# Moving the table load, the ranking and the weight conversions in a fused attention, expert and gated-product kernel

## The chip, the core and the metric

The kernel runs on one core of a Trainium2 chip. The metric is the device time of one execution in microseconds (us). Three executions of the kernel before took 904.47, 911.55 and 910.23 us; the median is 910.23 us.

## What is computed

Three layers follow each other. The first is a gated linear attention with 4 batches, 8 heads, 768 steps and head width 48. The second sends each of the 3072 tokens to one of 8 experts (two matrices 384x1024 and 1024x384). The third is a gated product with 1536 hidden columns.

```python
f = 1 / (1 + exp(-f_logit))
for t in range(S):                                   # attention
    state = f[:, :, t, :, None] * state + einsum('bhd,bhe->bhde', k[:, :, t], v[:, :, t])
    y[:, :, t] = einsum('bhd,bhde->bhe', q[:, :, t], state)
logits = xn @ en.T / tau                             # routing, x and expert rows normalised
expert_idx = argmax(logits); gate_w = softmax(logits)[expert_idx]
for e in range(E):
    out[mask] = gate_w[mask] * (relu(x[mask] @ w1[e]) @ w2[e])
return ((x @ w_a) * (x @ w_b)) @ w_out               # gated product
```

## The kernel before

The order of the instructions on each engine is the order in which the program writes them; every engine works through its own list in order. DMAs are issued from SP's and ACT's lists, the scatters from POOL's.

**Attention.** The time axis is cut into 24 blocks g (6 chunks of 128 steps times 4 batches). `load_a(g)` fetches q, k and f of a block in two halves, one issued by SP and one by ACT; `load_b(g)` fetches two forms of v on SP. `prep_f(g)` makes the forget gates on ACT (a Tanh and a Copy), `prep_s(g)` runs two scans and five other operations on DVE, which make `kt` and `qc`. `pe(g)` is the block's PE work: the products `pp` of block g+2, the part of `y(g)` that comes from the state (`inter`), the part from within the block (`intra`), the products `kv` of block g+1 and the state's update `u_ps`. `evac(g)` copies y out of PSUM and squares it for the norm. In the loop, block g sees `prep_f(g+4)`, `prep_s(g+3)` and `pe(g)`. Ahead of the loop stand the constants, `warm_up` matmuls on a zero tile, `prep_f(0..3)`, `prep_s(0..2)` and two `pe` calls.

**Routing.** After the blocks 3, 7, 11, 15, 19, 21 and 23, `route` ranks the tokens of the round. It is a generator: `tick` writes its next piece between the pieces of `prep_s` and `pe`. `until(k)` holds it back until the loop counter `it` has reached the round's block plus k; `it` is raised by one for each block, and by a half in the middle of `pe`. Its matmuls `rk` give the positions, `pz`, `pos` and further small DVE operations follow, then the gate; `scale_row` and `scatter_row` write the rows to DRAM by expert.

**Experts.** 64 steps (8 experts, 8 slices of hidden columns): `h_part`, `h_split`, `y_part`. Products are made in three passes from a high and a low part of each operand, so the weights are converted: ACT makes the high part, POOL or DVE subtracts it to get the low part.

**Gated product.** 72 steps (6 tiles of 512 tokens, 12 slices of hidden columns). `ab_part(s)` makes two products `pa`, multiplies them on DVE (`rows`, L913) and splits the result into `gh` (ACT) and `gl` (DVE); `q_part(s-1)` is the second product, whose passes take `gh` and `gl` of the step before. The gated weights come as 64-bit numbers; `job_run` converts one half piece in three stages, each advanced by `w_next`: an Abs on ACT and three DVE operations, two DVE operations, then the high part on ACT and the low part (`lo`, L691) on POOL. Nine of the eighteen half pieces are converted in the first gated steps.

Of the kernel before, what the change touches and what calls it, by code (L numbers as in the profile page):

```python
# [6 lines left out]
F32 = mybir.dt.float32  # L7
F32R = mybir.dt.float32r
BF16 = mybir.dt.bfloat16
I32 = mybir.dt.int32  # L10
ACTF = mybir.ActivationFunctionType
# [38 lines left out]
def build(tc, I, out, dbg=None):  # L50
# [12 lines left out]
    ident = const.tile([128, 128], F32, name="ident")  # L63
    off_i = const.tile([1, NE], I32, name="off_i")
    ones = const.tile([128, 128], BF16, name="ones")
    warm = const.tile([128, 512], BF16, name="warm")
    flag_i = const.tile([1, 1], I32, name="flag_i")
    flag_b = const.tile([1, 1], BF16, name="flag_b")
    fl_sb = const.tile([128, 1], F32, name="fl_sb")
# [49 lines left out]
    with tc.manual_schedule():  # L119
# [178 lines left out]
        def warm_up(n):  # L298
            wp = ps_kv.tile([128, 512], F32, tag="kv", name="wp")
            for i in range(n):  # L300
                T.matmul(out=wp, lhsT=ones, rhs=warm, start=(i == 0), stop=(i == n - 1))

        def pe(g):
            n = g + 2
# [26 lines left out]

        def evac(g, y, rd):
            i = len(rd["x"])
            yx = x_p.tile([128, H, VW], F32, tag="yx", name="yx", bufs=7)
            A.activation(out=yx, in_=y, func=ACTF.Copy)
            junk = x_p.tile([128, H, D], BF16, tag="junk", name="junk", bufs=1)
            A.activation(out=junk, in_=yx[:, :, 0:D], func=ACTF.Square, accum_out=rd["ssq"][:, i:i + 1])
            late.append(lambda: V.tensor_reduce(out=rd["lg"][:, i], in_=yx[:, :, D:VW].rearrange("p h e -> p e h"),
                                                axis=AX.X, op=ALU.add))
            rd["x"].append((g, yx))  # L340
# [5 lines left out]
        def route(rd, i0):  # L346
            nb = len(rd["x"])
            lg, ssq = rd["lg"][:, 0:nb], rd["ssq"][:, 0:nb]
            rt = lambda nm, w=NE, dt=F32: r_p.tile([128, B, w], dt, tag=nm, name=nm)[:, 0:nb]
            bc = lambda t: t.to_broadcast([128, nb, NE])  # L350
            prio_b = prio.unsqueeze(1).to_broadcast([128, nb, NE])

            def until(k):
                while it[0] < i0 + k:
                    yield

            yield from until(1)
            nrm = rt("nrm", 1)
            G.tensor_tensor(out=nrm[:, :, 0], in0=ssq, in1=half[:, 0:nb], op=ALU.pow)
            mx = rt("mx", 1)  # L360
            V.tensor_reduce(out=mx, in_=lg, axis=AX.X, op=ALU.max)
            yield
            eq = rt("eq")
            V.tensor_tensor(out=eq, in0=lg, in1=bc(mx), op=ALU.is_ge)
            z = rt("z")
            V.tensor_tensor(out=z, in0=lg, in1=bc(mx), op=ALU.subtract)
            yield
            V.tensor_tensor(out=eq, in0=eq, in1=prio_b, op=ALU.mult)
            yield
            m2 = rt("m2", 1)  # L370
            V.tensor_reduce(out=m2, in_=eq, axis=AX.X, op=ALU.max)
            yield
            oh = rt("oh", NE, BF16)
            V.tensor_tensor(out=oh, in0=eq, in1=bc(m2), op=ALU.is_equal)
            yield from until(2)
            ps = ps_r.tile([128, B, NE], F32, tag="r", name="rk")[:, 0:nb]
            T.matmul(out=ps, lhsT=tri, rhs=oh, start=True, stop=False, skip_group_check=True)
            T.matmul(out=ps, lhsT=ones[0:1], rhs=base[:, 0:nb], start=False, stop=False, skip_group_check=True)
            T.matmul(out=ps, lhsT=ones, rhs=run.unsqueeze(1).to_broadcast([128, nb, NE]),
                     start=False, stop=(nb == 1), skip_group_check=True)  # L380
            for i in range(nb - 1):
                T.matmul(out=ps[:, i + 1:nb], lhsT=ones,
                         rhs=oh[:, i:i + 1].to_broadcast([128, nb - 1 - i, NE]),
                         start=False, stop=(i == nb - 2), skip_group_check=True)
            V.tensor_scalar(out=nrm, in0=nrm, scalar1=1e-6, scalar2=None, op0=ALU.add)
            yield
            V.reciprocal(out=nrm, in_=nrm)
            yield
            V.tensor_tensor(out=z, in0=z, in1=bc(nrm), op=ALU.mult)
            yield from until(2.5)  # L390
            A.activation(out=z, in_=z, func=ACTF.Tanh, scale=0.5)
            yield
            pz = rt("pz")
            V.tensor_tensor(out=pz, in0=ps, in1=oh, op=ALU.mult)
            yield
            pos = rt("pos", 1)
            V.tensor_reduce(out=pos, in_=pz, axis=AX.X, op=ALU.add)
            yield
            seen = r_p.tile([128, NE], F32, tag="seen", name="seen")
            V.tensor_reduce(out=seen, in_=oh.rearrange("p i e -> p e i"), axis=AX.X, op=ALU.add)  # L400
            yield
            V.tensor_tensor(out=run, in0=run, in1=seen, op=ALU.add)
            yield
            posi = r_p.tile([128, B, 1], I32, tag="posi", name="posi", bufs=4)[:, 0:nb]
            V.tensor_copy(posi, pos)
            yield from until(3)
            den = rt("den")
            V.tensor_scalar(out=den, in0=z, scalar1=-1.0, scalar2=1.0, op0=ALU.mult, op1=ALU.add)
            yield
            V.reciprocal(out=den, in_=den)  # L410
            yield
            V.scalar_tensor_tensor(out=den, in0=z, scalar=1.0, in1=den, op0=ALU.add, op1=ALU.mult)
            yield
            gate = rt("gate", 1)
            V.tensor_reduce(out=gate, in_=den, axis=AX.X, op=ALU.add)
            yield
            V.tensor_scalar(out=gate, in0=gate, scalar1=1e-9, scalar2=None, op0=ALU.add)
            yield
            V.reciprocal(out=gate, in_=gate)
            for i, (g, yx) in enumerate(rd["x"]):  # L420
                scq.append((g, yx, gate[:, i], posi[:, i]))
# [56 lines left out]
        SP.dma_start(out=en_bd, in_=I["embbd"])  # L478
        tau = ob_p.tile([128, 1], F32, name="tau")
        V.memset(half, 0.5)  # L480
        V.memset(ones, 1.0)
        V.memset(warm, 0.0)
        V.memset(qkf_t[1], 0.0)
# [4 lines left out]
        SP.dma_start(out=tau, in_=I["tau"].to_broadcast([128, 1]))  # L488
        load_b(0)
        load_a(2)  # L490
        load_b(1)
        load_a(3)
        load_b(2)
        load_a(4)
        A.activation(out=half, in_=half, func=ACTF.Tanh, scale=0.0, bias=0.0)
        V.memset(half, 0.5)
        onesf = raw0[:, 512:640]
        emb8 = raw0[:, 1024:1216].rearrange("p (k w) -> p k w", k=KC)
# [12 lines left out]

        warm_up(12)
        prep_f(0)
        prep_f(1)
        V.tensor_tensor(out=emb8, in0=en_bd, in1=en_bd, op=ALU.mult)
        pe_ps = ps_r.tile([128, H, NE], F32, tag="r", name="en_ps")
# [3 lines left out]
        prep_s(0)  # L520
        V.tensor_reduce(out=en, in_=pe_ps.rearrange("p h e -> p e h"), axis=AX.X, op=ALU.add)
        G.tensor_tensor(out=en, in0=en, in1=half, op=ALU.pow)
        prep_f(2)
        prep_s(1)
        V.tensor_scalar(out=en, in0=en, scalar1=1e-6, scalar2=tau, op0=ALU.add, op1=ALU.mult)
# [141 lines left out]
        def job_run(n, c, raw):  # L667
# [17 lines left out]
            V.scalar_tensor_tensor(out=r0, in0=r0, scalar=29, in1=ct, op0=ALU.logical_shift_right, op1=ALU.bitwise_xor)  # L685
            yield
            V.scalar_tensor_tensor(out=r0, in0=r1, scalar=-2147483648, in1=r0, op0=ALU.bitwise_and, op1=ALU.bitwise_xor)
            V.tensor_scalar(out=r0, in0=r0, scalar1=0x40000000, scalar2=None, op0=ALU.bitwise_xor)
            yield
            A.activation(out=hi, in_=as3(r0), func=ACTF.Copy)  # L690
            G.tensor_tensor(out=lo, in0=as3(r0), in1=hi.bitcast(F32), op=ALU.subtract)  # L691

        running = []

        def w_start(s, lag):
            if not running and loaded:
# [191 lines left out]
        def ab_part(s):  # L888
# [10 lines left out]
            for at in range(0, XT, n):  # L899
                r = slice(at, at + n)  # L900
                pp = []
                for i in range(2):
                    wh, wl = w_get(32 + 3 * (f // 4) + i, KC)
                    pa = ps_ab.tile([128, XT], F32, tag=f"ab{i}", name="pa")[:, r]
                    for k in range(KC):
                        mm3(pa, wh[:, k, c], wl[:, k, c], XH[tt][0][:, k, r], XH[tt][1][:, k, r], k == 0, k == KC - 1)
                    pp.append(pa)
                    if i == 0:
                        A.activation(out=ab[:, r], in_=pa, func=ACTF.Copy)  # L909
                        if at == 0:  # L910
                            w_next()
                            job_load(s)
                V.tensor_tensor(out=ab[:, r], in0=ab[:, r], in1=pp[1], op=ALU.mult)  # L913
                A.activation(out=gh[:, r], in_=ab[:, r], func=ACTF.Copy)  # L914
                V.tensor_tensor(out=gl[:, r], in0=ab[:, r], in1=gh[:, r].bitcast(F32), op=ALU.subtract)  # L915

        def q_open(tt):
            QS[tt] = [ps_o.tile([128, CAP], F32, tag="o", name="pq")[:, 0:DM] for _ in range(4)]
# [28 lines left out]
        def q_part(s):  # L947
# [7 lines left out]
            for i in range(4):  # L955
# [3 lines left out]
                if f == F2J - 1:  # L959
                    q_out(tt, i)  # L960

        for s in range(NTT * F2J + 1):
            tt, f = divmod(s, F2J)
            ab_part(s)
# [3 lines left out]
                y_part(NE * FJ - 1)  # L968
            q_part(s - 1)
            w_start(NE * FJ + s, 1)  # L970
            if running:
                w_next()
                w_next()
        gctx.close()
        ectx.close()

# [200 lines left out]
```

## Time and profile before

| what | before |
|---|---|
| median of three executions | 910.23 us |
| the profiled execution | 909.4 us |
| its span | 907.7 us |
| PE busy | 873.2 us, 96% |
| DVE busy | 428.2 us, 47% |
| ACT busy | 336.8 us, 37% |
| POOL busy | 237.5 us, 26% |

The profiled execution took 909.4 us, of which the span from the first to the last instruction is 907.7 us. PE is the engine with the most work, so the time is PE's work plus the stretches in which PE waits or runs at its lower clock. Busy shares hide these; they are read stage by stage.

### The profile page before, as it was taken

What the parts mean: (1) busy time and instruction counts of PE and PEld (TensorE: products, weight loads), DVE (VectorE), ACT (ScalarE), POOL (GpSimd) and SP (SyncE); (2) the same over time, 40 slices, a digit from 0 to 9 for tenths busy, and PEclk for the clock granted to TensorE, in tenths of its full rate; (3) what the DMA queues carried; (4) which work ended last, traced back from release to release, by engine and by line L of the source; (5) the groups of instructions that cost most, each with busy time, mean ns of one, the idle gap of its engine ahead of it and who ended that gap; (6) DMA issues with size and microseconds to landing.
All of it is one profiled execution on the core that took longest, in us unless ns stands there. A gap on an engine that the chain in (4) does not pass through costs nothing. (4 is left out here: it accounts for less than half of the span.)

```text
span 907.7 us, 12520 instructions
## 1 busy us (share of the span) xinstructions
PE 873.2 (96%) x4888; PEld 772.0 (85%) x4893; DVE 428.2 (47%) x791; ACT 336.8 (37%) x609; POOL 237.5 (26%) x223
## 2 busy tenths in 40 slices
PE   5999999969999999999999899999999999999996
PEld 2789898849999999999887788888888888888885
DVE  5998999533443544355788622222222222222221
ACT  2666777424344444444344222222222212212211
POOL 3334555564346434642222210010001001001001
PEclk6999999669999999999999999999999999999998
DMA  9789897223545455542333100000000000000001
GB/s 198 184 214 235 216 224 205 104 75 101 154 152 174 130 152 159 170 126 85 104 105 104 36 35 1 1 35 0 1 5 31 1 1 35 0 1 36 1 1 37
DMA packets 39861, 82.34 MB, mean 91 GB/s; under 512 B 4716, under 2 KB 22084, under 8 KB 39796
## 3 DMA queue, kind: packets, MB, share of 16 engines
q1 hardware_dynamic: 35156, 64.82, 25.5%
q10 hardware_dynamic: 1568, 7.18, 3.4%
q0 software_dynamic: 3072, 9.49, 3.1%
q8 instruction: 40, 0.66, 0.3%
q14 instruction: 25, 0.20, 0.1%
HBM read 69.57 MB, written 11.90 MB: 90 GB/s over the span
## 5 line engine op out<-in xcount | busy, mean ns | idle before, releaser
L764 PE MATMUL pa<-a,w 128*128 128x512 f32 (+1 forms) x438 | 170.5, 389 | 0.0
L763 PE MATMUL pa<-a,w 128*128 128x512 f32 (+1 forms) x438 | 170.4, 389 | 0.0
L762 PE MATMUL pa<-a,w 128*128 128x512 f32 (+1 forms) x438 | 169.0, 386 | 0.0
L913 DVE TENSOR_TENSOR rows<-rows,pa 128x512 f32<-128x512 f32 (+1 forms) x73 | 49.6, 680 | 242.6 <-PE pa L764 242.6
L940 POOL DMA_INDIRECT out<-yT,idx x24 | 23.4, 974 | 363.8 <-ACT yT L938 358.3
L909 ACT ACTIVATE rows<-pa 128x512 f32<-128x512 f32 (+1 forms) x73 | 43.2, 591 | 164.7 <-PE pa L764 164.4
L928 PE MATMUL pq<-w,gl 128*128 128x384 f32 x288 | 97.5, 339 | 2.8 <-DVE gl L915 2.7
L673 POOL TENSOR_TENSOR w<-raw,w 128x512 fp32r<-128x512 f32 x56 | 84.9, 1536 | 54.5 <-ACT w L670 51.9
L914 ACT ACTIVATE gh<-rows 128x512 fp32r<-128x512 f32 (+1 forms) x73 | 45.6, 625 | 143.9 <-DVE rows L913 143.9
L926 PE MATMUL pq<-w,gh 128*128 128x384 f32 x288 | 97.0, 337 | 0.8 <-ACT gh L914 0.8
L927 PE MATMUL pq<-w,gh 128*128 128x384 f32 x288 | 96.8, 336 | 0.3 <-POOL w L691 0.3
L764 PEld LDWEIGHTS pa<-a,w 128*128 128x128 f32 x438 | 82.2, 188 | 16.9
L763 PEld LDWEIGHTS pa<-a,w 128*128 128x128 f32 x438 | 82.2, 188 | 15.4
L762 PEld LDWEIGHTS pa<-a,w 128*128 128x128 f32 x438 | 82.3, 188 | 15.1
L815 PE MATMUL po<-hh,w 128*128 128x448 f32 x384 | 90.1, 370 | 0.0
L915 DVE TENSOR_TENSOR gl<-rows,gh 128x512 fp32r<-128x512 f32 (+1 forms) x73 | 60.0, 822 | 52.1 <-ACT gh L914 52.1
L785 DVE SCALAR_TENSOR_TENSOR hl<-ph,hh 128x448 fp32r<-128x448 f32 x64 | 39.9, 624 | 87.6 <-ACT hh L784 87.0
L784 ACT ACTIVATE hh<-ph 128x448 fp32r<-128x448 f32 x64 | 34.9, 546 | 124.3 <-PE ph L764 124.2
L815 PEld LDWEIGHTS po<-hh,w 128*128 128x128 f32 x384 | 70.5, 188 | 5.4 <-ACT hh L784 0.4
L762 PE MATMUL ph<-a,w 128*128 128x448 f32 x192 | 71.0, 370 | 0.0
L763 PE MATMUL ph<-a,w 128*128 128x448 f32 x192 | 70.5, 367 | 0.0
L764 PE MATMUL ph<-a,w 128*128 128x448 f32 x192 | 70.4, 367 | 0.0
(162 smaller groups left out, 1420.1 us busy)
## 6 DMA issues: line engine op xcount, KB each, us to landing
raw<-moe_w SPq DMA_DIRECT2D x32, 768.0 KB, 4.6
qkf<-qkf SPq DMA_DIRECT2D x24, 288.0 KB, 6.7
qkf<-qkf ACTq DMA_DIRECT2D x24, 288.0 KB, 4.3
vx<-vx SPq DMA_DIRECT2D x24, 224.0 KB, 4.4
rows<-slots SPq DMA_DIRECT2D x7, 679.0 KB, 6.2
vT<-vT SPq DMA_DIRECT2D x24, 192.0 KB, 4.6
raw<-moe_w_a SPq DMA_DIRECT2D x6, 768.0 KB, 4.7
raw<-moe_w_b SPq DMA_DIRECT2D x6, 768.0 KB, 4.5
```

Of the source, the lines that this page charges most:

```text
L673: (G if i < NPOOL else V).tensor_tensor(out=wt[:, 1, f], in0=raw[:, f], in1=wt[:, 0, f].bitcast(F32), op=ALU.subtract)
L762: T.matmul(out=out, lhsT=wh, rhs=xh, start=first, stop=False)
L763: T.matmul(out=out, lhsT=wl, rhs=xh, start=False, stop=False)
L764: T.matmul(out=out, lhsT=wh, rhs=xl, start=False, stop=last)
L815: T.matmul(out=OS[e][k], lhsT=w[:, j % 4, k * 128:(k + 1) * 128], rhs=x, start=(j == 0 and w is wh and x is hh), stop=(j == FJ - 1 and x i ...
L909: A.activation(out=ab[:, r], in_=pa, func=ACTF.Copy)
L913: V.tensor_tensor(out=ab[:, r], in0=ab[:, r], in1=pp[1], op=ALU.mult)
L914: A.activation(out=gh[:, r], in_=ab[:, r], func=ACTF.Copy)
L915: V.tensor_tensor(out=gl[:, r], in0=ab[:, r], in1=gh[:, r].bitcast(F32), op=ALU.subtract)
L926: T.matmul(out=q, lhsT=gh[:, c], rhs=wh[:, f % 4], start=(f == 0), stop=False)
L927: T.matmul(out=q, lhsT=gh[:, c], rhs=wl[:, f % 4], start=False, stop=False)
L928: T.matmul(out=q, lhsT=gl[:, c], rhs=wh[:, f % 4], start=False, stop=(f == F2J - 1))
```

## The change

- The Tanh that makes ACT load its table stands ahead of the DMA issues of `load_a(1)`; the loads of blocks 1 (v), 3, 2 (v) and 4 are written after `prep_f(0)` and after `prep_s(0)`.
- `route` holds the ranking matmuls back to it = block + 2.5, the middle of `pe`, where it was block + 2, ahead of `pe`.
- The squares of `evac` go to the PSUM tile of y, where they went to a bfloat16 tile in SBUF; `yx` has 8 buffers (7 before). The warm-up's zero tile is one column, read 512 times.
- In the gated product the stages of a conversion stand between and after the step's own operations; the low part is made by DVE, where POOL made it; one DVE operation of the second stage moves to the third.

```diff
-    warm = const.tile([128, 512], BF16, name="warm")
+    warm = const.tile([128, 2], BF16, name="warm")
...
-                T.matmul(out=wp, lhsT=ones, rhs=warm, start=(i == 0), stop=(i == n - 1))
+                T.matmul(out=wp, lhsT=ones, rhs=warm[:, 0:1].to_broadcast([128, 512]), start=(i == 0), stop=(i == n - 1))
...
-            yx = x_p.tile([128, H, VW], F32, tag="yx", name="yx", bufs=7)
+            yx = x_p.tile([128, H, VW], F32, tag="yx", name="yx", bufs=8)
             A.activation(out=yx, in_=y, func=ACTF.Copy)
-            junk = x_p.tile([128, H, D], BF16, tag="junk", name="junk", bufs=1)
-            A.activation(out=junk, in_=yx[:, :, 0:D], func=ACTF.Square, accum_out=rd["ssq"][:, i:i + 1])
+            A.activation(out=y[:, :, 0:D], in_=yx[:, :, 0:D], func=ACTF.Square, accum_out=rd["ssq"][:, i:i + 1])
...
-            yield from until(2)
+            yield from until(2.5)
...
         V.memset(half, 0.5)
+        A.activation(out=half, in_=half, func=ACTF.Tanh, scale=0.0, bias=0.0)
...
         load_b(0)
         load_a(2)
-        load_b(1)
-        load_a(3)
-        load_b(2)
-        load_a(4)
-        A.activation(out=half, in_=half, func=ACTF.Tanh, scale=0.0, bias=0.0)
         V.memset(half, 0.5)
...
         prep_f(0)
+        load_b(1)
+        load_a(3)
         prep_f(1)
...
+        load_b(2)
+        load_a(4)
         prep_f(2)
...
             V.scalar_tensor_tensor(out=r0, in0=r1, scalar=-2147483648, in1=r0, op0=ALU.bitwise_and, op1=ALU.bitwise_xor)
+            yield
             V.tensor_scalar(out=r0, in0=r0, scalar1=0x40000000, scalar2=None, op0=ALU.bitwise_xor)
-            yield
             A.activation(out=hi, in_=as3(r0), func=ACTF.Copy)
-            G.tensor_tensor(out=lo, in0=as3(r0), in1=hi.bitcast(F32), op=ALU.subtract)
-
-        running = []
+            low_by[0].tensor_tensor(out=lo, in0=as3(r0), in1=hi.bitcast(F32), op=ALU.subtract)
+
+        running, low_by = [], [G]
...
                         A.activation(out=ab[:, r], in_=pa, func=ACTF.Copy)
-                        if at == 0:
-                            w_next()
-                            job_load(s)
                 V.tensor_tensor(out=ab[:, r], in0=ab[:, r], in1=pp[1], op=ALU.mult)
                 A.activation(out=gh[:, r], in_=ab[:, r], func=ACTF.Copy)
+                if at == 0:
+                    w_next()
                 V.tensor_tensor(out=gl[:, r], in0=ab[:, r], in1=gh[:, r].bitcast(F32), op=ALU.subtract)
+            w_next()
+            job_load(s)
...
+        low_by[0] = V
         for s in range(NTT * F2J + 1):
...
             w_start(NE * FJ + s, 1)
-            if running:
-                w_next()
-                w_next()
+            w_next()
```

ACT at the start of the program, before (the number behind `qkf_` is the buffer: 131 is block 0, 135 block 4; `F` are the forget gates):

```order
L172 DMA qkf_131<-qkf 48x1536
L477 DMA qkf_131<-zgap 16x1536
L172 DMA qkf_132<-qkf 48x1536
L172 DMA qkf_133<-qkf 48x1536
L172 DMA qkf_134<-qkf 48x1536
L172 DMA qkf_135<-qkf 48x1536
L495 ACT_TABLE_LOAD
L495 ACTIVATE half<-half 128x8
L186 ACTIVATE F_129<-qkf_131 128x4x128
```

and after the change:

```order
L172 DMA qkf_131<-qkf 48x1536
L476 DMA qkf_131<-zgap 16x1536
L480 ACT_TABLE_LOAD
L480 ACTIVATE half<-half 128x8
L172 DMA qkf_132<-qkf 48x1536
L172 DMA qkf_133<-qkf 48x1536
L186 ACTIVATE F_129<-qkf_131 128x4x128
L187 ACTIVATE F_129<-F_129 128x4x128
L172 DMA qkf_134<-qkf 48x1536
L186 ACTIVATE F_130<-qkf_132 128x4x128
```

The table load stands two DMAs ahead of the first gates, where it stood behind six, and the DMA of block 3 stands behind the first gates.

PE in the blocks 20 and 21, where the round of block 19 is ranked (`rk`), before:

```order
L233 MATMUL kv<-en_bd,vT 128x64 x3
L295 MATMUL y<-vx,pm 128x56 x6
L377 LDWEIGHTS tri
L377 MATMUL rk<-oh,tri 128x32
...
L382 MATMUL rk<-oh,ones 128x8
L252 MATMUL pp<-qc,kt 128x128 x8
L286 MATMUL y<-S_126,qc 128x112 x4
```

and after the change:

```order
L295 MATMUL y<-vx,pm 128x56 x6
L252 MATMUL pp<-qc,kt 128x128 x8
L286 MATMUL y<-S_126,qc 128x112 x4
L233 MATMUL kv<-en_bd,vT 128x64 x3
L376 LDWEIGHTS tri
L376 MATMUL rk<-oh,tri 128x32
...
L381 MATMUL rk<-oh,ones 128x8
L295 MATMUL y<-vx,pm 128x56 x6
```

The ranking matmuls (four more of them stand between the two rows shown) moved from ahead of `pp` to behind `kv` of the same block.

DVE in one gated step with a conversion, before:

```order
L913 TENSOR_TENSOR rows<-rows,pa 128x512
L915 TENSOR_TENSOR gl<-rows,gh 128x512
L682 TENSOR_SCALAR ct<-ct 128x768
L683 TENSOR_SCALAR ct<-ct 128x768
L685 SCALAR_TENSOR_TENSOR raw<-raw,ct 128x768
L687 SCALAR_TENSOR_TENSOR raw<-raw 128x768
L688 TENSOR_SCALAR raw<-raw 128x768
```

and after the change:

```order
L909 TENSOR_TENSOR rows<-rows,pa 128x512
L686 SCALAR_TENSOR_TENSOR raw<-raw 128x768
L913 TENSOR_TENSOR gl<-rows,gh 128x512
L688 TENSOR_SCALAR raw<-raw 128x768
L690 TENSOR_TENSOR w_68<-raw,w_68 128x768
L681 TENSOR_SCALAR ct<-ct 128x768
L682 TENSOR_SCALAR ct<-ct 128x768
L684 SCALAR_TENSOR_TENSOR raw<-raw,ct 128x768
```

DVE's list has one operation more in a step, the low part (L690), and it stands ahead of the next conversion's first stage.

## Rows read from the trace of the kernel before

**Rows 1.** Busy time by stage (stretch; us, busy, clock, DMA share, GB/s).
```profile
0.00:30.00 30.00, 17.83 (x86) 9.06 (x87) 19.45 (x41) 8.92 (x17) 10.10 (x20) 0.77 0.90 188
30.00:162.00 132.00, 131.82 (x1236) 118.84 (x1239) 122.93 (x280) 91.08 (x212) 61.01 (x76) 1.00 0.84 215
162.00:200.00 38.00, 28.34 (x144) 23.22 (x145) 14.08 (x79) 12.60 (x31) 21.06 (x30) 0.64 0.29 92
...
443.00:517.00 74.00, 70.06 (x331) 59.86 (x330) 59.49 (x71) 29.70 (x45) 18.77 (x10) 1.00 0.28 86
517.00:900.00 383.00, 382.18 (x1861) 337.24 (x1859) 97.61 (x149) 86.45 (x148) 22.01 (x23) 1.00 0.03 12
```

**Rows 2.** Timeline of ACT at the start (start us, us, operation [idle before]).
```profile
1.27 0.44 ACTq L477 DMA_DIRECT2D qkf<-zgap  x1
...
11.44 1.28 ACT L495 ACT_TABLE_LOAD   x1 [11.44 <-DMA qkf<-qkf]
...
13.79 0.63 ACT L186 ACTIVATE F<-qkf 128x512 f32<-128x512 f32 x1 [0.85 <-DVE F L503]
```

**Rows 3.** Timeline of DVE at the start.
```profile
3.27 1.34 DVE L484 MEMSET qkf<- 128x1536 f32 x1 [0.27 <-issue]
13.01 0.07 DVE L496 MEMSET half<- 128x8 f32 x1 [8.40 <-ACT half L495]
...
15.70 1.22 DVE L200 TENSOR_TENSOR_SCAN Bt<-F,pat 128x516 f32<-128x516 f32 x1
```

**Rows 4.** DMA issues of 1.2 to 1.7 and 2.5 to 4 us (us to landing last).
```profile
qkf<-zgap ACTq DMA_DIRECT2D x1, 96.0 KB, 6.1
...
qkf<-qkf ACTq DMA_DIRECT2D x1, 288.0 KB, 7.5
```

**Rows 5.** Timeline of PE, first products of the loop.
```profile
30.13 1.05 PE L252 MATMUL pp<-qc,kt 64*128 64x128 f32 x14
```

**Rows 6.** Timeline of DVE and PE at the ranking of block 19's round.
```profile
162.42 0.94 DVE L216 TENSOR_TENSOR qc<-qkf,Rt 128x512 f32<-128x512 f32 x1
163.28 0.61 DVE L374 TENSOR_TENSOR oh<-eq,m 128x32 bf16<-128x32 f32 x1
...
163.94 0.18 PE L377 MATMUL rk<-oh,tri 128*128 128x32 bf16 x1 [1.96 <-DVE oh L374]
```

**Rows 7.** Busy time of two microseconds behind that ranking, columns as in Rows 1.
```profile
166.00:168.00 2.00, 2.00 (x11) 2.00 (x11) 0.00 (x0) 0.00 (x0) 1.01 (x2) 0.50 0.77 222
```

**Rows 8.** Timeline: a block's `qc`, the `pp` that takes it, a wait for `rk`.
```profile
96.46 0.69 DVE L216 TENSOR_TENSOR qc<-qkf,Rt 128x512 f32<-128x512 f32 x1
...
98.42 1.16 PE L252 MATMUL pp<-qc,kt 64*128 64x128 f32 x16
...
178.79 0.17 DVE L394 TENSOR_TENSOR pz<-rk,oh 128x16 f32<-128x16 f32 x1 [2.86 <-PE rk L382]
```

**Rows 9.** Timeline of one gated step with a conversion.
```profile
481.05 0.68 DVE L913 TENSOR_TENSOR rows<-rows,pa 128x512 f32<-128x512 f32 x1
481.17 0.90 ACT L690 ACTIVATE w<-raw 128x768 fp32r<-128x768 f32 x1 [4.20 <-DVE raw L688]
...
482.15 1.89 POOL L691 TENSOR_TENSOR w<-raw,w 128x768 fp32r<-128x768 f32 x1 [5.26 <-ACT w L690]
...
482.62 1.96 DVE L915 TENSOR_TENSOR gl<-rows,gh 128x512 fp32r<-128x512 f32 x1 [0.89 <-ACT gh L914]
...
488.20 0.68 DVE L913 TENSOR_TENSOR rows<-rows,pa 128x512 f32<-128x512 f32 x1
```

**Rows 10.** Timeline of DVE in gated steps without a conversion.
```profile
521.33 0.69 DVE L913 TENSOR_TENSOR rows<-rows,pa 128x512 f32<-128x512 f32 x1 [4.29 <-PE pa L764]
522.72 0.69 DVE L915 TENSOR_TENSOR gl<-rows,gh 128x512 fp32r<-128x512 f32 x1 [0.70 <-ACT gh L914]
527.56 0.69 DVE L913 TENSOR_TENSOR rows<-rows,pa 128x512 f32<-128x512 f32 x1 [4.15 <-PE pa L764]
```

**Rows 11.** Groups by line: one DVE conversion operation (busy us, mean ns; idle before).
```profile
L685 DVE SCALAR_TENSOR_TENSOR raw<-raw,ct 128x768 int32<-128x768 int32 x18 | 17.3, 959 | 1.6
```

## The prediction

> **What bounds the kernel.** I read the busy time by stage first, because a busy share over the whole span hides where PE idles. From 30 to 162 us (the attention's loop) PE is busy 131.82 of 132 us, and from 517 us to 900 us it is busy all but 0.8 us [rows 1]. There the change can win only by making PE's work begin earlier. PE's lost time is in three places. At the start PE is busy 17.83 of 30 us, partly with warm-up matmuls. At the attention's end the clock averages 0.64 of full speed and PE also waits. In the first gated steps it loses 3.94 of 74 us [rows 1]. The change touches all three. Then I read the timelines of the engines that end the waits there.
>
> At the start, ACT issues six DMAs, some of them held back until older transfers have landed, and comes to the table load only at 11.44 us [rows 2]. DVE stands still for 8.40 us until ACT has rewritten `half`, and only then clears the tiles that the first gates need; the gates begin at 13.79 and the first scan at 15.70 [rows 2, 3].
>
> **The start: -6.9 us.** Now the table load follows the second DMA issue, so it begins at 1.27 + 0.44 = 1.7 and ends at 3.0; `half` is ready before DVE ends its second large memset at 3.27 + 1.34 = 4.6 [rows 2, 3]. DVE's wait is gone. What is late next is the data of block 0: its last piece is issued at 1.27 and lands 6.1 us later, at 7.4 [rows 2, 4]. Two gate operations of 0.63 give 8.7, so the first scan starts at about 8.8 instead of 15.70: 6.9 us. The next gates want block 1, issued at 3.0 and landing 7.5 us later: 10.5, plus 1.3 for the gates is 11.8, while its scan is wanted at 4.25 us after the first, 13.0 [rows 4]. So the chain of scans moves as a whole, and the loop's first `pp`, at 30.13 before, starts at 23.2 [rows 5]. From there on PE is full, so the whole gain is kept unless something else runs dry. That something is DMA: its engines are 0.90 busy in the first 30 us and 0.84 in the loop [rows 1]. ACT also issues block 2 later, since it now waits for a transfer of block 0 (about 7.4), and lands it by about 15; its gates end at 16.5 and its scan is wanted near 18.4. The cover is 1.9 us there. Ends: -7.5 (PE's warm-ups also shorten) and half of it, -3.5, if DMA sets the pace of the first blocks; I take -6.9 because every landing that I can work out comes before its use.
>
> **The ranking: -0.5 us.** Of seven rounds, the one of block 19 makes PE wait 1.96 us for `oh`, with `pp` behind it in the queue [rows 6]. What `pp` itself needs, `qc`, is ready at 162.42 + 0.94 = 163.36, `rk` starts at 163.94 [rows 6]. Now `pp` starts at 163.4, and `rk` comes some 3 us later, when `oh` is long done (163.28 + 0.61). The wait shrinks from 1.96 to about 1.4 us. In the other rounds PE is full on either side, so the order costs nothing. Ends: 0 and -1.96.
>
> **The gated steps: -1.4 us.** A step without a conversion takes PE 527.56 - 521.33 = 6.23 us [rows 10]. With one, DVE needs 488.20 - 481.05 = 7.15 [rows 9], falls behind by 0.9 a step, and in the end PE waits for `gl`. In these 7.15 us stand `rows` 0.68, 0.89 idle because ACT makes the high part before `gh`, `gl` 1.96, and five conversion operations, 488.20 - 484.58 = 3.62. `gl` alone takes 0.69 [rows 10]; here it ends only 0.54 after POOL's low part (482.15 + 1.89) [rows 9]. The change takes away the idle 0.89 and the 1.27 on `gl`. It adds the low part on DVE, which no row shows: DVE's conversion operation of 768 columns with two inputs takes 0.96 [rows 11], POOL's low part 1.89 [rows 9]; I take 0.96, the same engine and size. It also adds a wait, for the high part on ACT (0.90 [rows 9]), with the next conversion queued behind it. Sum 0.68 + 3.62 + 0.69 + 0.96 + 0.90 = 6.85 at most, about 6.7 as neighbours overlap a little. But conversions now begin in step 0, one step sooner: eight spacings of 6.7, 53.6 us, against six of 7.15 and two of about 6, 55, and step 0 loses about 1 us more to the experts' last copies. So DVE reaches its last conversion no earlier. What remains is that `gl` ends 0.68 + 0.96 + 0.69, less overlap 2.2, behind the start of `rows` instead of 3.53: -1.4 us of the 3.94. Ends: -3.9 (all waiting gone) and +5 (the low part at POOL's 1.89, some 0.9 us over eight steps less the `gl` gain).
>
> **The rest: 0.** Squares into PSUM take the place of squares into SBUF on ACT, which is 69% busy in the loop (91.08 of 132) and has two y tiles to work with; nine low parts leave POOL, which nothing waits for; the smaller zero tile saves 0.2 us ahead of the start's long wait. PE covers the experts' moved operation (the step's own results are used one product later). If that cover went, ACT would be late by less than 1 us a conversion.
>
> **Sum.** Against the profiled 909.4 (span 907.7): 909.4 - 6.9 - 0.5 - 1.4 = 900.6 us. The profiled execution lies 0.8 us below the median of 910.23, well inside the spread of the three runs.
>
> **The clock, and the rivals.** Behind the 1.96 us wait PE's granted clock is 0.50 (1.2 GHz): eleven matmul records in 2 us [rows 7], where the loop has 1236 in 132, 18.7 in 2 us, at 2.4 GHz [rows 1]. It stays low to the attention's end. The three runs are 904.47, 910.23 and 911.55: I read the first as an execution in which it did not fall, worth about 6.4 us. The Trainium skill ("TensorE: Matmul & The Clock Gate", Part 1) calls the monitor's window free-running, so that where a change lands differs from run to run; the spread of these runs agrees, and no row here shows the runs' own clocks.
> - A, the forecast: the clock still falls behind the shorter wait: 900.6 us. Chance 0.48.
> - B, it mostly stays at 2.4 GHz, since PE waits 1.4 us instead of 1.96: 900.6 - 6.4 = 894.2. For it speaks the run of 904.47 even with the long wait, against it that three of four executions before (with the profiled one) fell. Chance 0.32.
> - C, half the start's gain goes to DMA: 904.1. The 0.90 share speaks for it, the landings against it. Chance 0.10.
> - D, the low part costs DVE 1.89, so DVE lags more than before: 900.6 + 1.4 + 5 = 907, within 1%. Chance 0.05.
> - E, slower: `pz` now waits. `rk` comes later on PE, `pz` stands ahead of the next block's scan on DVE, and DVE is 93% busy in the loop (122.93 of 132). One such wait before was 2.86 us [rows 8]; five full rounds of it are 14.3, of which little is covered if DVE is no more than 1 us ahead: 900.6 + 14.3 = 914.9. It decides if DVE reaches `pz` before PE has passed `kv`. Against it: `qc` ends at 97.15 and the `pp` that takes it starts at 98.42 [rows 8], so when DVE is through with `qc`, PE is in the last 1.3 us of the block, past `rk`. Chance 0.05.
>
> That the change does not do what it says could be at the start alone, if the first gates waited for something other than `half`; that is in C.
>
> **Numbers.** The forecast is A's 900.6. The range reaches from B less 2.7 us (the start at -7.5, the gated steps at -3.5) to C plus 1.4 (no gated gain): 891.5 to 905.5; outside lie D, E and the tails, under 2 in 10. A measurement can tell about 1% (9.1 us) from no change, so "faster" means below 901.1: all but a little of B and somewhat over half of A, 0.60. Within 1%: the rest of A, C and D, 0.35. Slower: 0.05.
>
> **What would show it.** The table load near 1.7 us, the first scan near 8.8, the loop's first `pp` near 23.2 and no wait of PE in the loop. The ranking's wait on PE gone and about 1.4 us ahead of `pp` in block 21 in its place; the clock behind it tells A from B. `gl` at 0.69 and `rows` 6.6 to 6.9 us apart in the conversion steps, with PE idle 2.5 us there. It is wrong if gates wait for DMA in the first ten blocks, if `pz` idles, or if the conversion steps are 7.2 us apart or more.

## The result, and the profile after

Four executions of the changed kernel took 896.56 to 902.56 us, median 900.41; the kernel before, run beside them, 909.23. The ratio is 0.9894 (95% interval 0.986 to 0.9927). A second set of twelve executions has a median of 902.83 against 909.49 and a ratio of 0.9942 (0.9914 to 0.9969). So the change wins 0.6 to 1.1%, at the edge of what a measurement of this kernel can tell. The profiled execution took 900.34 us, its span is 898.6. Its total is the forecast's, its parts are not. Busy time by stage in the changed kernel, columns as in [rows 1]:

```profile
0.00:23.00 23.00, 17.04 (x86) 8.08 (x87) 19.43 (x41) 8.81 (x16) 9.96 (x20) 0.93 0.96 200
23.00:155.00 132.00, 129.59 (x1208) 116.09 (x1210) 121.44 (x270) 90.16 (x208) 55.82 (x73) 1.00 0.87 219
155.00:193.00 38.00, 31.54 (x166) 26.33 (x167) 17.65 (x89) 14.00 (x34) 19.76 (x32) 0.60 0.26 89
...
436.00:508.00 72.00, 70.50 (x336) 61.07 (x335) 57.27 (x83) 31.60 (x47) 1.88 (x1) 1.00 0.31 96
```

The loop starts 7 us sooner, but in 132 us of it PE now idles 2.4 us, where it idled 0.2 [rows 1]. Where the two timelines of PE stand at the same operation says what each stretch gave or took:

| PE reaches | before | after | ahead by | this stretch |
|---|---|---|---|---|
| the loop's first `pp` (block 2) | 30.13 | 23.25 | 6.88 | -6.88 |
| `pp` of block 22 | 157.33 | 153.71 | 3.62 | +3.26 |
| `pp` of block 23 | 164.35 | 159.99 | 4.36 | -0.74 |
| the experts' first product (`pt`) | 199.03 | 195.37 | 3.66 | +0.70 |
| the gated product's step 0 | 443.27 | 438.17 | 5.10 | -1.44 |
| its step 11 | 516.94 | 508.66 | 8.28 | -3.18 |
| end of the last product | 899.18 | 890.90 | 8.28 | 0 |
| end of the span | 907.7 | 898.6 | 9.06 | -0.78 |

The last stretch, from PE's end to the last output's landing, is 7.6 to 8.7 us in all fourteen traces and follows none of the edits: spread.

**The start** came as worked out. The changed kernel's timeline, of ACT, DVE and PE:

```profile
1.75 1.28 ACT L480 ACT_TABLE_LOAD   x1 [1.75 <-PEq L1169]
...
7.29 0.63 ACT L186 ACTIVATE F<-qkf 128x512 f32<-128x512 f32 x1 [4.04 <-DMA qkf<-zgap]
...
8.61 1.23 DVE L200 TENSOR_TENSOR_SCAN Bt<-F,pat 128x516 f32<-128x516 f32 x1 [0.86 <-ACT F L187]
...
14.81 0.63 ACT L186 ACTIVATE F<-qkf 128x512 f32<-128x512 f32 x1 [3.25 <-DMA qkf<-qkf]
...
23.25 1.16 PE L252 MATMUL pp<-qc,kt 64*128 64x128 f32 x16
```

The first gates no longer wait for DVE's clearing but for block 0's last transfer (4.04 us), as named. Those of blocks 2, 3 and 4 wait for theirs too (3.25, 3.32 and 1.22 us), yet the scans of the first eight blocks stay 7.0 to 7.1 us ahead of their old places.

**The loop** gives 3.26 us back. PE's waits between 24 and 165 us (us in total, times, longest); before there was one, `rk`'s 1.96 [rows 6]:

```profile
PE pp L252 <- DVE qc L216: 1.5, 1, 1.5
PE pp L252 <- ACT F L186: 1.0, 1, 1.0
PE pp L252 <- ACT xr L433: 0.7, 1, 0.7
PE pp L252 <- ACT w L106: 0.4, 1, 0.4
```

Three of the four name an ACT operation, but `pp` reads `qc` and `kt` from DVE; `qc` of block 21 starts at 145.38 on DVE's timeline and its `pp` at 146.64. The cause stands seven microseconds earlier, in the ranking of block 15's round:

```profile
138.19 0.15 DVE L384 TENSOR_SCALAR nrm<-nrm 128x4 f32<-128x4 f32 x1
...
138.59 0.19 DVE L388 TENSOR_TENSOR z<-z,nrm 128x32 f32<-128x32 f32 x1
138.81 0.23 ACT L390 ACTIVATE z<-z 128x32 f32<-128x32 f32 x1 [1.81 <-DVE z L388]
138.95 0.58 ACT L262 ACTIVATE pm<-pp 128x512 f32<-128x512 f32 x1
140.52 0.61 ACT L106 ACTIVATE w<-raw 128x512 fp32r<-128x512 f32 x1
141.16 0.69 DVE L114 TENSOR_TENSOR w<-raw,w 128x512 fp32r<-128x512 f32 x1 [0.86 <-ACT w L106]
...
145.38 1.12 DVE L216 TENSOR_TENSOR qc<-qkf,Rt 128x512 f32<-128x512 f32 x1
...
146.64 1.25 PE L252 MATMUL pp<-qc,kt 64*128 64x128 f32 x16 [1.01 <-ACT F L186]
```

The scale `nrm`, its reciprocal and the product `z` follow the ranking's matmuls in `route` and so moved with them. Before, they stood half a block ahead of the Tanh, which waited for nothing:

```profile
141.15 0.19 DVE L389 TENSOR_TENSOR z<-z,nrm 128x32 f32<-128x32 f32 x1
...
142.43 0.23 ACT L391 ACTIVATE z<-z 128x32 f32<-128x32 f32 x1
```

Now ACT stands 1.81 us at the Tanh, with `pm`, the copy of y and the weight's high part queued behind it; DVE then waits 0.86 for that high part, and a DVE that is 92% busy in the loop does not make it up. The round of block 11 shows the same (1.22 and 0.85 us). From scan to scan (138.92 to 147.32 us) DVE takes 8.40 us, 1.54 more than before; it is busy 7.39 of them, where it was 6.58, so the wait is only part of it.

**The gated steps** gained 3.18 us. Between `rows` and the next `rows` of a conversion step:

```profile
463.75 0.68 DVE L909 TENSOR_TENSOR rows<-rows,pa 128x512 f32<-128x512 f32 x1
...
465.22 0.68 DVE L913 TENSOR_TENSOR gl<-rows,gh 128x512 fp32r<-128x512 f32 x1
...
467.39 0.96 DVE L690 TENSOR_TENSOR w<-raw,w 128x768 fp32r<-128x768 f32 x1 [1.01 <-ACT w L689]
...
470.33 0.68 DVE L909 TENSOR_TENSOR rows<-rows,pa 128x512 f32<-128x512 f32 x1
```

The low part costs 0.96 and waits 1.01 for the high part, `gl` is down to 0.68 from 1.96 [rows 9], and the spacing is 6.58. Most spacings are 6.5 to 6.6, at the lower edge of the forecast's 6.6 to 6.9; the first is 7.37, and the one in which the next tile is split 8.34 (before 9.02). PE's waits there sum to 1.4 us (before 3.8), 2.4 less; the other 0.8 us of the gain stand in no wait that the profile shows.

**The clock.** Behind `pp` of block 23, which waits 1.55 us, the granted clock falls as it did before:

```profile
162.00:166.00 4.00, 4.00 (x25) 3.85 (x25) 0.00 (x0) 0.34 (x2) 2.45 (x3) 0.50 0.87 253
```

It is at 0.50 (1.2 GHz) until about 191 us. The kernel before has a second such stretch at the experts' start (0.50 from 200 to 202 us) and the changed kernel has 1.00 there, which is most of the 1.44 us gained ahead of step 0. That is chance: in the second profiled execution of the changed kernel (e12) it is back, 0.53 from 198 to 200 us.

### The profile page after: what moved, and what is told of

Read it like the earlier page. It is cut to its first block, busy times and chain, and to the rows that moved or that the text cites. A ratio compares the mean times of both kernels' runs of the same rounds, so it can differ in the third digit from the quotient of the medians.

```text
span 898.6 us, 12526 instructions
## 1 busy us (share of the span) xinstructions
PE 872.6 (97%) x4888; PEld 771.0 (86%) x4893; DVE 424.5 (47%) x800; ACT 338.4 (38%) x609; POOL 217.6 (24%) x214
## 5 line engine op out<-in xcount | busy, mean ns | idle before, releaser
L814 PEld LDWEIGHTS po<-hh,w 128*128 128x128 f32 x384 | 70.5, 188 | 5.3 <-ACT hh L783 0.4
L913 DVE TENSOR_TENSOR gl<-rows,gh 128x512 fp32r<-128x512 f32 (+1 forms) x73 | 49.9, 684 | 44.3 <-ACT gh L910 44.3
```

The lines of the kernel that those rows point to most:

```text
L814: T.matmul(out=OS[e][k], lhsT=w[:, j % 4, k * 128:(k + 1) * 128], rhs=x, start=(j == 0 and w is wh and x is hh), stop=(j == FJ - 1 and x i ...
```

## The experiments

Theory R: the scale and `z`, moved with the ranking, give back the loop's 3.3 us. Theory L: the moved loads, or a VectorE without slack, do. Theory C: the clock falls because PE stands empty ahead of block 23. Each run has one trace; a stretch of it is compared, and the total of the executions behind it. The diffs are shortened, and the comments in them are this text's. "Loop" is from `pp` of block 2 to that of block 22; "last blocks" from `pp` of block 23 to the copy of y(23); "eleven steps" from step 0 to step 11 of the gated product (the recorded expectation of e9 calls the latter step 10).

| kernel | first `pp` | loop | last blocks | eleven steps | median us | ratio to before (95%) |
|---|---|---|---|---|---|---|
| before | 30.13 | 127.20 | 19.64 | 73.67 | 908.8 to 910.1 | 1 |
| change, first set | 23.25 | 130.46 | 20.57 | 70.49 | 900.41 | 0.9894 (0.986-0.9927) |
| change, e12 | 23.82 | 130.46 | 21.13 | 70.45 | 902.83 | 0.9942 (0.9914-0.9969) |
| e1, start alone | 23.60 | 127.20 | 20.06 | 73.76 | 904.61 | 0.9936 (0.9912-0.996) |
| e2, ranking alone | 30.21 | 130.47 | 14.39 | 73.75 | 910.64 | 1.0016 (0.9987-1.0046) |
| e3, gated alone | 29.60 | 127.20 | 15.05 | 70.46 | 905.62 | 0.9956 (0.9927-0.9986) |
| e4, without the ranking | 23.90 | 127.21 | 20.58 | 70.49 | 901.86 | 0.9932 (0.9905-0.996) |
| e5, scale and z early | 23.77 | 128.78 | 20.56 | 70.48 | 899.42 | 0.989 (0.9842-0.9939) |
| e6, hole filled | 23.59 | 130.49 | 14.31 | 70.56 | 896.42 | 0.9873 (0.9835-0.9911) |
| e7, low part on GpSimd | 23.77 | 130.49 | 15.92 | 77.51 | 908.47 | 1.0011 (0.9983-1.0039) |
| e8, loads as before | 28.83 | 130.47 | 16.19 | 70.48 | 907.54 | 1.0004 (0.9979-1.0029) |
| e9, old order, low part on VectorE | 23.62 | 130.48 | 20.39 | 78.71 | 911.03 | 1.0023 (1.0-1.0047) |
| e10, e5 and filled | 24.17 | 127.58 | 13.78 | 70.53 | 893.63 | 0.9829 (0.9791-0.9867) |
| e11, e4 and filled | 24.19 | 132.04 | 13.35 | 70.50 | 894.19 | 0.9837 (0.9802-0.9873) |

The totals that the expectations reckon from the changed kernel's 900.4 us came out 1 to 7 us above what the theory that held had given, but for e10's; the changed kernel's own second set is 2.4 us above. So the stretches decide below, and the totals only where their intervals part.

**e1, the start alone** (before with the change's start):

```diff
+A.activation(out=half, in_=half, func=ACTF.Tanh, scale=0.0, bias=0.0)   # ahead of the memsets
-load_b(1); load_a(3); load_b(2); load_a(4)                              # ahead of prep_f(0)
-A.activation(out=half, in_=half, func=ACTF.Tanh, scale=0.0, bias=0.0)   # behind these loads
+load_b(1); load_a(3)                                                    # behind prep_f(0)
+load_b(2); load_a(4)                                                    # behind prep_s(0)
```

> The kernel before with the start's part alone: the table load ahead of the memsets and the loads of blocks 1 to 4 behind the first gates and the first scans. The start is 6.9 us shorter in the changed kernel's trace, yet at the end of the last attention block only 3.4 us are left. Theory R (the later ranking is what gives 3.4 us back: its scale and its Tanh now follow one another, ScalarE waits for VectorE, and VectorE falls behind): here the ranking stands where it stood, so the loop keeps the start's gain; 909.2 - 6.9 = 902.3 us, no TensorE wait between 23 and 155 us. Theory L (the loads moved behind the gates, or a VectorE that has no slack for an earlier start, give it back): 909.2 - 3.4 = 905.8 us, with waits for qc in blocks 17 to 23.

The loop starts at 23.60 and takes 127.20 us as before: it keeps all 6.5 us, and theory L falls. The total, 5.5 us at the medians, is less than the 6.9; in this trace the experts take 2.1 us longer than before, which no edit explains (last section).

**e2, the ranking alone** (before with this line, the eighth `yx` buffer, the Square into PSUM and the narrow warm tile):

```diff
-yield from until(2)
+yield from until(2.5)
```

> The kernel before with the later ranking alone (its matmuls half a block later), together with the eighth yx buffer, the Square into PSUM and the narrow warm tile, without which the rows held longer find no buffer. Theory R: the loop loses about 3.4 us to waits for qc in blocks 17 to 23, and the 1.96 us wait of the ranking becomes one of 1.5 us: 909.2 + 3.0 = 912.2 us. Theory L: the loop loses nothing here, the wait shortens by 0.4 us: 908.8 us. The prediction's term for it was -0.5 us (908.7).

The loop takes 130.47 us, +3.27 with the old start: theory R. The total does not resolve it (interval -0.1 to +0.5%).

**e3, the gated part alone** (before with the diff's pieces in `job_run`, `ab_part` and the last loop):

```diff
-G.tensor_tensor(out=lo, ...)
+low_by[0].tensor_tensor(out=lo, ...)      # low_by[0] = V ahead of the gated steps
+w_next()                                  # behind gh, at step's end; w_next(); job_load(s) behind gl
```

> The kernel before with the gated product's part alone (one conversion step behind gh, one behind gl, one at the step's end, the low part of a weight's split on VectorE, the exclusive-or one stage later). The changed kernel's trace has eight gated steps that are 0.6 to 0.94 us shorter, 3.2 us together: 906.0 us if that is this part's own. The prediction's term for it was -1.4 us: 907.8. If the spacing of those steps came from the earlier stages, nothing: 909.2.

The eleven steps take 70.46: the part's own -3.2 us, and 905.62 against 906.0 expected.

**e4, the change without the later ranking**:

```diff
-yield from until(2.5)
+yield from until(2)
```

> The changed kernel with the ranking's matmuls back where they were, all else as changed. Theory R: the loop keeps its 6.9 us, the ranking's wait of 1.96 us is back: 900.4 - 3.4 + 0.4 = 897.4 us. Theory L: 900.4 + 0.4 = 900.8 us.

The loop is back at 127.21, and between 23 and 155 us PE never idles:

```profile
23.00:155.00 132.00, 132.00 (x1237) 118.42 (x1237) 122.14 (x280) 91.36 (x212) 59.27 (x75) 1.00 0.89 222
```

But the median, 901.86, is no better than the change's (the intervals overlap widely), and the 897.4 of theory R did not come. In this trace the 2.6 us of lead over the changed kernel at `pp` of block 22 are 1.8 at that of block 23, behind the wait of 1.96 us for `oh` that is back, 0.95 at the experts' first product, and none at step 0 of the gated product, since the clock falls again at the experts' start (0.50 from 196 to 198 us). So in this trace the loop's gain is lost in one wait, in 0.9 us between block 23 and the experts that no run explains, and in one stretch of low clock, which comes and goes from trace to trace.

**e5, scale and z early**: only these three operations stand at `until(2)`; matmuls and Tanh at 2.5.

```diff
+yield from until(2)
+V.tensor_scalar(out=nrm, ...); yield; V.reciprocal(out=nrm, in_=nrm); yield; V.tensor_tensor(out=z, ...)
 yield from until(2.5)
 T.matmul(out=ps, lhsT=tri, rhs=oh, ...)
-V.tensor_scalar(out=nrm, ...); yield; V.reciprocal(...); yield; V.tensor_tensor(out=z, ...)
-yield from until(2.5)
 A.activation(out=z, in_=z, func=ACTF.Tanh, scale=0.5)
```

> The changed kernel with the ranking's matmuls half a block later as changed, but the scale and its product with z (three VectorE operations) left where they stood, ahead of them. The ranking is late, only ScalarE's Tanh no longer follows the product at once. If the wait of ScalarE for that product is what gives 3.4 us back in the loop (theory R in its narrow form), pp(18) to pp(22) stand 3 us earlier than in the changed kernel: pp(22) at about 151, and TensorE waits for qc before pp(23) alone; 900.4 - 3.4 = 897.0 us. If the later matmuls themselves do it, pp(22) stays at about 153.7 and 900.4 us.

At the same place neither ACT nor, after it, DVE waits:

```profile
137.23 0.23 ACT L390 ACTIVATE z<-z 128x32 f32<-128x32 f32 x1
...
139.49 0.61 ACT L106 ACTIVATE w<-raw 128x512 fp32r<-128x512 f32 x1
...
140.53 0.68 DVE L114 TENSOR_TENSOR w<-raw,w 128x512 fp32r<-128x512 f32 x1
```

The loop takes 128.78, of which 1.2 are in its first block, where the clock was low (0.60 from 24 to 27 us); from block 3 to 22 it is 121.86, against 121.47 before and 124.73 changed. The narrow form holds: 2.9 of the 3.3 us came from the three operations in front of the Tanh, 0.4 stay with the later matmuls. The total, 899.42, cannot be told from the change's.

**e6, the hole filled**:

```diff
 p_open(n)
+if g == NG - 3:
+    warm_up(7)
 for p in range(NP): p_part(n, p)
```

> The changed kernel with seven warming matmuls more on TensorE ahead of pp(23), where it waits 1.55 us. Theory C (the granted clock falls because TensorE stands empty there): it stays at full there, the last three blocks of y take some 14 us from pp(23) instead of 20.6 (the kernel with the later ranking alone kept its clock and took 14.4), all behind it comes 6.2 us earlier: 900.4 - 6.2 = 894.2 us in nearly all runs. Rival: the clock falls for another reason than this wait, such as the thinner work of the last blocks: it falls at about 161 us as it did, 900.4 to 900.8 us.

The seven matmuls fill the hole to the last tenth, and the clock stays up until 170 us:

```profile
158.65 1.69 PE L301 MATMUL wp<-warm,ones 128*128 128x512 bf16 x7
160.28 1.16 PE L252 MATMUL pp<-qc,kt 64*128 64x128 f32 x16
```

```profile
162.00:166.00 4.00, 4.00 (x41) 3.91 (x40) 0.31 (x2) 1.95 (x6) 3.38 (x4) 1.00 0.75 232
166.00:170.00 4.00, 3.40 (x33) 3.24 (x32) 3.37 (x21) 2.10 (x6) 1.90 (x8) 1.00 0.29 114
170.00:174.00 4.00, 4.00 (x21) 3.81 (x20) 1.81 (x11) 2.47 (x8) 3.09 (x4) 0.52 0.28 101
```

The last blocks take 14.31 us instead of 20.57; of these 6.3 us, 4.7 are left at the end of PE's work (886.24 against 890.90). All six executions of e6, and all twelve of e10 and e11, have a mean clock of 0.983 to 0.991; the change's twelve on e12's chip have 0.975 to 0.981. Theory C holds in this form: where the hole is filled, the clock does not fall there. The kernel before shows that with the hole the fall is likely and not certain: 64 of its 80 executions have 0.975 or less (median 910.2 us) and 16 have 0.979 or more (904.9). In the traces a hole of 1.5 to 2.0 us at this place was followed by the long stretch at 0.50 in seven of the eleven unfilled ones. That it is the emptiness that decides, and not the work that the seven matmuls add, is not shown: no run closes the hole in another way.

The Trainium skill ("TensorE: Matmul & The Clock Gate", What's actually happening) says that the moment at which the clock rises varies, by where in the monitor's window the first matmul lands. These runs vary too, at the fall; they do not show the reason.

**e7, the low part on GpSimd** in the new order, and **e9, the old order with the low part on VectorE**, both on the change:

```diff
-low_by[0] = V                             # e7
+low_by[0] = G
-w_next()                                  # e9: behind gh, behind gl and at the step's end
+w_next(); job_load(s)                     # e9: behind the copy of the first pa,
+if running: w_next(); w_next()            # and at the step's end; the xor in the second stage
```

> The changed kernel with the low part of a weight's split in the gated product on GpSimd, as it was, and the new order of the conversions kept. If the order alone shortened the eight gated steps, they start 6.2 to 6.6 us apart as in the changed kernel: 900.4 us. If the engine did (gl took 1.96 us beside a running GpSimd and 0.69 without), the steps with a conversion are 6.9 to 7.2 us apart again: 900.4 + 2 to 3 = 902.4 to 903.4 us. The prediction took half of each.

> The changed kernel with the gated product's conversion steps ordered as before and only the low part of the split left on VectorE; with the kernel that has the new order and GpSimd's low part it completes the square. From the start of step 0 to the start of step 10 the traces have 73.7 us with neither, 70.5 us with both and 77.5 us with the order alone. If the engine is what gains and the order only spreads the work, 70.5 to 71.5 us and a time of 900.4 to 901.4 us; if VectorE's low part needs the new order so as not to stand ahead of the product with pa that gh waits for, 74 to 76 us and 904 to 906 us.

The eleven steps take 73.7 us with neither edit, 77.5 with the order alone, 78.7 with the engine alone, 70.5 with both: in these steps each alone is worse than nothing, and by more than either expectation allowed. In e7 GpSimd's low part lies beside DVE's first operation of the next piece, which takes 1.57 instead of 0.55 us, and the next `rows` waits behind it:

```profile
473.97 1.89 POOL L690 TENSOR_TENSOR w<-raw,w 128x768 fp32r<-128x768 f32 x1 [5.60 <-ACT w L689]
474.71 1.57 DVE L681 TENSOR_SCALAR ct<-ct 128x768 f32<-128x768 f32 x1 [1.74 <-ACT ct L680]
477.84 0.68 DVE L909 TENSOR_TENSOR rows<-rows,pa 128x512 f32<-128x512 f32 x1
```

The Trainium skill ("SBUF — State Buffer", Who interferes with whom) has VectorE and GpSimd share one pair of ports, which, where both want it, the first to issue holds for its whole instruction. The trace agrees: DVE's operation ends at 476.28, 0.42 us after GpSimd's. In e9 the low part stands ahead of `rows`, with its wait for ACT's high part, and PE waits 5.7 us for `gh` (first line, of PE's waits; below it DVE's timeline):

```profile
PE pq L925 <- ACT gh L913: 5.7, 5, 2.6
...
479.92 0.96 DVE L690 TENSOR_TENSOR w<-raw,w 128x768 fp32r<-128x768 f32 x1 [0.95 <-ACT w L689]
480.80 0.68 DVE L912 TENSOR_TENSOR rows<-rows,pa 128x512 f32<-128x512 f32 x1
...
482.23 0.69 DVE L914 TENSOR_TENSOR gl<-rows,gh 128x512 fp32r<-128x512 f32 x1 [0.76 <-ACT gh L913]
```

**e8, the loads where they stood**, on the change:

```diff
 load_a(2)
+load_b(1); load_a(3); load_b(2); load_a(4)
 ...
 prep_f(0)
-load_b(1); load_a(3)
 ...
-load_b(2); load_a(4)
```

> The changed kernel with the table load early as changed, but the loads of blocks 1 to 4 issued where they stood, ahead of the first gates. If the early table load alone made the start shorter, the loop's first pp is at 23.3 and the time 900.4 us. If the loads ahead of the gates on ScalarE's queue hold the first gate (it then comes after the last of them, near 11.4 us, where the table load of the kernel before stood), only the table load's own time of 1.3 to 2.4 us is gained of the 6.9: the loop's first pp at 28 to 29 us, 900.4 + 4.5 to 5.6 = 904.9 to 906.0 us.

ACT's list holds three loads for 7.06 us, and the first gate comes behind them, for all that the table is there at 3.0:

```profile
5.82 7.06 ACTq L172 DMA_DIRECT2D qkf<-qkf  x3
13.00 0.63 ACT L186 ACTIVATE F<-qkf 128x512 f32<-128x512 f32 x1 [9.75 <-DMA vT<-vT]
```

The early table load is worth 1.3 of the 6.9 us; with the loads behind the gates they are all had. (The first `pp` of kernels with one and the same start differs by up to 0.9 us.)

**e10 and e11, combinations**: e10 is e5 with e6's two lines; e11 is e4 with

```diff
+if g == NG - 3:
+    warm_up(8)
 prep_s(g + 3)
```

> The changed kernel with both findings: the scale and the product with z where they stood, and seven warming matmuls ahead of pp(23). If the two losses are separate (3 us of loop from ScalarE's wait, 6 us from the clock), the loop's 3 us come on top of the 896.4 us of the filled kernel: 893.4 us, pp(22) at 151 to 152.5 and the granted clock at full until about 170 us. If what the loop gains is lost again while the rows are scattered and loaded, 896.4 us.

> The changed kernel without the later ranking, and eight warming matmuls ahead of the ranking's matmuls of block 21, where TensorE waits 1.96 us for VectorE. Theory C: which wait is filled does not matter, the clock stays at full through the last three blocks; pp(22) at 151, y(23) ended at about 173, 900.4 - 3.4 - 6.2 = 890.8 us at best and 893 if the start of the experts gives some back. If the later ranking is needed to keep the clock: 900 us.

Both beat the kernel before, e10 by 1.7%, and the changed kernel measured beside them (e12); in e10's trace PE never waits in the loop, `pp` of block 23 included. The 893.63 is close to the 893.4 that two separate losses predict. e11's profiled execution took 899.23 us, its median is 894.19. In that trace the clock was low in the loop's first ten microseconds, and 4.8 us went there. Waits of 2.00 and 1.84 us stand ahead of it at the start; the changed kernel's trace has such waits too, 2.02 and 1.15, and kept its clock:

```profile
24.00:34.00 10.00, 9.82 (x53) 9.04 (x53) 5.97 (x12) 5.15 (x12) 2.18 (x4) 0.51 0.81 202
```

**e12, the change again**, with no edit:

> The changed kernel itself, on the chip of these three, so that they can be told from it: 900.4 us, its loop with the waits for qc ahead of pp(17), pp(21), pp(22) and pp(23) as before (theory R says that they are the order's own, not chance).

The same four waits at the same blocks, and a loop of 130.46 us to the hundredth; 902.83 us.

## Why the prediction came out

- **The start, -6.9: right** (-6.88). The price was that of all its edits together; that the loads, not the table load, carry about 5.6 of it, the prediction did not separate. ACT issued block 2 at 5.82, not at 7.4 as reckoned; that it landed by 14.8, near the forecast's 15, is luck.
- **The ranking, -0.5: wrong.** It was +2.5 (loop +3.26, the wait ahead of block 23 -0.74). The step that failed is "In the other rounds PE is full on either side, so the order costs nothing". That followed `rk` alone. What stands behind `rk` in the generator moved too: three DVE operations right in front of an ACT operation that has the loop's work queued behind it. Rival E looked for a late `pz`; it idled 0.2 us in the loop, and 4.3 and 2.5 us behind it (before 2.9).
- **The gated steps, -1.4: right in mechanism, mis-sized** (-3.2). Spacing, `gl` and the low part are as worked out; the term that "DVE reaches its last conversion no earlier" left 2.5 us of waiting, and 1.4 us remained. (The 3.53 less 2.2 of its last step is 1.3, not 1.4.)
- **The rest, 0:** -1.5 us, from the second stretch of low clock and the last output (-1.44, -0.78) less 0.70 ahead of the experts: chance, as the other traces show.
- **The clock:** A held in the profiled execution; another of the first four, 896.56 us at a mean clock of 0.984, looks like B. B's price, 6.4 us, is close to the 6.3 us that e6 takes from the last blocks; the two groups of the kernel before are 5.3 us apart. B's condition, a shorter wait, was not enough: behind 1.54 or 1.55 us of waiting the long fall came in four of seven traces, behind 1.96 or 1.97 in three of four. With the wait filled it came in none of three.
- **The signs:** "no wait of PE in the loop" failed, by the ranking's four waits. Gates did wait for DMA in the first ten blocks, which was to show the forecast wrong; that sign was badly set, since a gate that waits costs nothing while its scan comes in time.

Summed, -6.88 + 2.52 + 0.70 - 1.44 - 3.18 - 0.78 = -9.06: the total of 900.6 was met by luck, because errors cancelled: the ranking cost 3.0 us more than forecast, the gated steps gave 1.8 more and the rest 1.5. The 901.1 below which "faster" was to lie stands between the two sets, 900.41 and 902.83.

## What to carry to other kernels

When a step of a generator is held back, follow every operation behind it to the next engine's list: a small one placed right in front of its reader stops all that is queued there. An empty stretch of PE of 1.5 us can cost four times its length through the clock, as ahead of the last blocks here, and in the three kernels that filled it with a few idle matmuls the clock did not fall there. Two edits on one contended stretch may be worth less than nothing apart and much together; test the square.

## What was not expected

The experts' steps that convert nothing new take 3.65 us in most traces and 3.72 in some, with the granted clock at 1.00 in both: in e2 all through, in e1 from the 15th on, in e5 for five early steps. From the experts' first product to step 0 of the gated product that makes 247.8 us in e2 and 246.3 in e1, against 244.2 before. Nothing in the traces tells why, and no run here tests it; it blurs the totals, which is why stretches were compared here.
